# Every second ELU gate on GpSimd, the first two head pairs in written order, the first queries loaded through ScalarE's queue, and five smaller weight-decoding buffers, in a fused top-k attention and ELU feed-forward kernel

## The chip, the cores and the metric

The kernel runs on one core of one Trainium2 chip. Its measure is the device time of one launch in microseconds (us). The core has four engines that compute, each with its own instruction stream that runs in order: PE (TensorE, the matmuls; PEld are its weight loads, which overlap with them), DVE (VectorE), ACT (ScalarE) and POOL (GpSimd). SP (SyncE) issues the DMAs of the kernel before. The engines meet only in semaphores: an instruction that waits holds up all that stands behind it on its engine.

## The reference, cut to what matters

```python
q, k, v: (8, 8, 576, 64)        # batch, heads, sequence, head dim
scores = (1/8) * q @ k.T
kth    = 32nd largest of each row
scores = where(scores >= kth, scores, -1e9)
attn   = softmax(scores)
x      = (attn @ v) as (4608, 512)
h      = x @ w_in               # (512, 2048)
g      = where(h > 0, h, exp(min(h, 0)) - 1)
out    = g @ w_out              # (2048, 512), fp32
```

All inputs but q, k and v come as float64 words: the two weight matrices are passed as pairs of 32-bit words and turned into fp32 on the chip.

## The kernel before

A step is 128 query rows of one head pair. There are 144 steps: 8 batches of 4 query tiles by 4 head pairs, and 2 more for the remaining 64 rows of each batch. The life of a step `u` is spread over the loop at L640: `scores(u)` is issued two steps ahead (PE matmuls L300 into the two PSUM tiles `wide`, copied and scaled by ACT at L308); `select`, or `select_row` in the first eight steps, finds the 32 largest of each row on DVE: for each of the two heads four MAX8 (L341, L353; L319, L329 in `select_row`) and three MATCH_REPLACE8 (L346; L323) over 576 columns. One step later `mask` takes two tiny POOL operations (`neg` L366, `gap` L368), then two ACT passes (L369, L370); `normalise` takes five tiny POOL operations (L380 to L385) and two POOL passes over 576 columns (L387). Then `turn` transposes the weights on PE (L406, copied by ACT at L407) and `attend` multiplies with v (L432); `finish` copies the result into the block's `xT` (L459).

The feed-forward part works on blocks of one to three slots of 128 tokens: five blocks of one slot in the first pair of batches, otherwise blocks of two and three. For each block `ffn_pieces` makes 16 pieces `hidden(f)` (four times two matmul records each, L490; three ACT passes, L502 to L504, into `n` and `gT`; the entry in the list `gates`) and four pieces `project(s, part)` for each slot (L513, eight matmul records each, from `gT` and `w_out`). The gate itself, `gT = gT + (n - 1)`, is one DVE scalar_tensor_tensor at L471, issued by `close_gates`: `feed`, called four times a step, closes the gates that were put in the list at least two calls before; `project` closes all that are left; `hidden` closes the oldest when more than three are open. There are 304 gates (19 blocks of 16). `feed` also decides from due times which pieces are issued where; these numbers are the same in both kernels.

The weights are decoded in 32 pieces of 128 x 512 numbers. `load_weight` (SP DMA of 512 KB into a tile of pool `raw`, three buffers of 4 x 512 words), `convert_first` (three ACT passes L169 to L171, one POOL tensor_scalar L172), `convert_last` (two DVE passes L179, L182, and one POOL integer add L186). `decode_piece(i)` asks for load i+2, does the first half of piece i and the last half of piece i-1. `hook` runs one of them four times a step inside `select_row`, so that they fill steps 0 to 7 (one more falls into step 8). When the last is issued, the pools of the decoding are closed and the late pools `f` (five buffers of `n`), `g` and `x` are opened in their place.

The order on PE, ACT, DVE and POOL is a scheduler's up to step 8 (`tight`); from there `manual_schedule` keeps the order as written. SP's stream holds all loads and stores: q and k of head pair 0, two weight pieces, q and k of head pair 1, v of pair 0, then the rest.

Of the kernel before, what the change touches and what calls it, by code (L numbers as in the profile page):

```python
# [8 lines left out]
AF = mybir.ActivationFunctionType  # L9
ALU = mybir.AluOpType  # L10
FP32 = mybir.dt.float32
U32 = mybir.dt.uint32
I32 = mybir.dt.int32
# [67 lines left out]
def kernel(  # L81
# [9 lines left out]
    nc = tc.nc  # L91
    P = nc.NUM_PARTITIONS
# [16 lines left out]
    def pool(name, bufs, **kw):  # L109
        return ctx.enter_context(tc.tile_pool(name=name, bufs=bufs, **kw))  # L110
# [5 lines left out]
    wkpool = pool("wk", 1)  # L116
    etpool = pool("et", 2)
    small = pool("small", 4)
    xtpool = pool("xt", 2)
    opool = pool("o", 1)  # L120
    ps_sc = pool("ps_sc", 1, space=PSUM)
    ps_t = pool("ps_t", 2, space=PSUM)
# [3 lines left out]
    raws = ExitStack()  # L126
    early = raws.enter_context(tc.tile_pool(name="early", bufs=1))
    earlyf = raws.enter_context(tc.tile_pool(name="earlyf", bufs=4))
    rawpool = raws.enter_context(tc.tile_pool(name="raw", bufs=3))

    ident = const.tile([P, P], FP32, tag="ident", name="ident")
    make_identity(nc, ident[:])
# [15 lines left out]
        return moe_w_out[f * P : (f + 1) * P, :], w_out[:, f, :]  # L148

    def load_weight(i):  # L150
        t = rawpool.tile([P, 4 * WN], U32, tag="raw", name="raw")
        nc.sync.dma_start(t[:, 0 : 2 * WN], weight(i)[0])
        raw[i] = t

    def parts(t):
        words = t[:, 0 : 2 * WN].rearrange("p (n w) -> p n w", w=2)
        return words[:, :, 0], words[:, :, 1], t[:, 2 * WN : 3 * WN], t[:, 3 * WN :]

    def convert_first(i):

        lo, hi, e, m = parts(raw[i])
        ef, mf = e.bitcast(FP32), m.bitcast(FP32)
        nc.scalar.activation(ef, hi.bitcast(FP32), AF.Abs, scale=2.0**-48)  # L169
        nc.scalar.activation(mf, lo, AF.Copy, scale=2.0**-29, bias=2.0**23)  # L170
        nc.scalar.activation(m.bitcast(I32), mf, AF.Copy, bias=-(2.0**23))  # L171
        nc.gpsimd.tensor_scalar(  # L172
            ef, ef, (2.0 - 2.0**-3 - 2.0**-23) * 2.0**-32, 2.0**-63, ALU.min, ALU.max
        )

    def convert_last(i):
        t, dst = raw.pop(i), weight(i)[1]
        lo, hi, e, m = parts(t)
        nc.vector.tensor_scalar(  # L179
            e, e, 0x0FFFFFFF, 3, ALU.bitwise_and, ALU.logical_shift_left  # L180
        )
        nc.vector.scalar_tensor_tensor(  # L182
            out=e, in0=hi, scalar=0x80000000, in1=e,
            op0=ALU.bitwise_and, op1=ALU.bitwise_or,
        )
        nc.gpsimd.tensor_tensor(  # L186
            dst.bitcast(I32), e.bitcast(I32), m.bitcast(I32), ALU.add
        )

    decode = []  # L190
# [2 lines left out]
    def hook():  # L193

        if not decode:
            return
        decode.pop(0)()
        if not decode:
            raws.close()
            late["f"] = ctx.enter_context(tc.tile_pool(name="f", bufs=5))  # L200
            late["g"] = ctx.enter_context(tc.tile_pool(name="g", bufs=2))
            late["x"] = ctx.enter_context(tc.tile_pool(name="x", bufs=2))

    def decode_piece(i):
        if i < 2 * NF:
            if i + 2 < 2 * NF:
                load_weight(i + 2)
            convert_first(i)
        if i > 0:
            convert_last(i - 1)  # L210
            decoded[0] = i

    loaded, kqT, vT = {}, {}, {}

    def load_qk(b, hp):

        for name, src in (("k", k), ("q", q)):
            n = J + 1 if name == "k" else J
            t = ldpool.tile([P, n, 2, D], FP32, tag=name + "in", name=name + "in")
            if name == "k":  # L220
                last = t
            for hh in range(2):
                nc.sync.dma_start(
                    t[:, 0:J, hh, :],
                    src[b, 2 * hp + hh, 0:JP, :].rearrange("(p j) d -> p j d", j=J),
                )
            nc.sync.dma_start(
                last[0:R, J, :, :] if name == "k" else last[R:P, J, :, :],
                src[b, 2 * hp : 2 * hp + 2, JP:S, :].rearrange("h p d -> p h d"),
            )  # L230
            loaded[b, hp, name] = t
# [47 lines left out]
    def start_qk(b, hp):  # L279
        turning.append(transpose_qk(b, hp))  # L280
# [171 lines left out]

    def finish(blk, parts, at, cols, src):
        if blk.xT is None:
            if blk.slots == 1 and late:
                blk.xT = late["x"].tile([P, NC, P], FP32, tag="xT", name="xT")
            else:
                blk.xT = xtpool.tile([P, NC, T], FP32, tag="xT", name="xT")
        nc.scalar.copy(blk.xT[:, at, cols], src)  # L459
        blk.left -= parts  # L460
        if blk.left == 0:
            ffn.extend(ffn_pieces(blk))
# [1 line left out]
    gates = []  # L464
    place = [0]

    def close_gates(keep=0):

        while gates and gates[0][0] <= place[0] - keep:
            _, dst, n = gates.pop(0)  # L470
            nc.vector.scalar_tensor_tensor(  # L471
                out=dst, in0=n, scalar=-1.0, in1=dst, op0=ALU.add, op1=ALU.add
            )

    def ffn_pieces(blk):
        n_tok = blk.slots * P

        def hidden(f):
            if f == 0 and blk.number == 0:
                g = early.tile([P, NF, P], FP32, tag="g", name="gT")  # L480
                blk.gT = [g[:, 0:NG], g[:, NG:NF]]
            elif f % NG == 0 and blk.number > 0:
                g = late["g"].tile([P, NG, T], FP32, tag="g", name="gT")
                blk.gT.append(g[:])
            if len(gates) > 3:
                gates[0] = (-1, *gates[0][1:])
                close_gates(place[0])
            ps = ps_f.tile([P, dm], FP32, tag="f", name="hps")
            for i in range(NC):
                nc.tensor.matmul(  # L490
                    ps[:, 0:n_tok],
                    w_in[:, i, f * P : (f + 1) * P],
                    blk.xT[:, i, 0:n_tok],
                    start=(i == 0),
                    stop=(i == NC - 1),
                )
            if blk.number == 0:
                n = earlyf.tile([P, P], FP32, tag="n", name="n")[:]
            else:
                n = late["f"].tile([P, T], FP32, tag="n", name="n")[:, 0:n_tok]  # L500
            g = blk.gT[f // NG][:, f % NG, 0:n_tok]
            nc.scalar.activation(n, ps[:, 0:n_tok], AF.Relu, scale=-1.0)  # L502
            nc.scalar.activation(g, ps[:, 0:n_tok], AF.Relu)  # L503
            nc.scalar.activation(n, n, AF.Exp, scale=-1.0)  # L504
            gates.append((place[0], g, n))

        def project(s, part):
            close_gates()
            if part == 0:
                blk.o = ps_f.tile([P, dm], FP32, tag="f", name="ops")  # L510
            step = NF // 4
            for f in range(part * step, (part + 1) * step):
                nc.tensor.matmul(  # L513
                    blk.o[:],
                    blk.gT[f // NG][:, f % NG, s * P : (s + 1) * P],
                    w_out[:, f, :],
                    start=(f == 0),
                    stop=(f == NF - 1),
                )
            if part == 3:  # L520
                o = opool.tile([P, dm], FP32, tag="osb", name="osb")
                nc.scalar.copy(o[:], blk.o[:])
                for t in blk.tiles[s]:
                    p0 = t.cols.start - s * P
                    nc.sync.dma_start(out[t.rows, :], o[p0 : p0 + t.ql, :])

        part = HIDDEN[blk.slots]
        behind = 2 * NF if blk.number else 0
        return [
            (part, max(behind, NC * (f // 4 + 1)), lambda f=f: hidden(f))  # L530
            for f in range(NF)
        ] + [
            (PROJECT, max(behind, NF + (part + 1) * NF // 4),
             lambda s=s, part=part: project(s, part))
            for s in range(blk.slots)
            for part in range(4)
        ]
# [75 lines left out]
            fed["sum"] += cost  # L613
            piece()

    load_qk(0, 0)
    for i in range(2):
        load_weight(i)
    load_qk(0, 1)
    load_v(0, 0)  # L620
    start_qk(0, 0)
    turn_qk(True)
    scores(steps[0])
    load_qk(0, 2)
    start_qk(0, 1)
    turn_qk(True)
    scores(steps[1])
    load_qk(0, 3)
    for hp in range(1, NHP):
        load_v(0, hp)  # L630
    decode += [lambda i=i: decode_piece(i) for i in range(2 * NF + 1)]
    at(0, start_qk, 0, 2)
    at(1, start_qk, 0, 3)

# [5 lines left out]
    for n in range(NS + 3):  # L640
# [20 lines left out]
                feed(n, 0.25)  # L661
            continue
        if n == tight:
            E = mybir.EngineType
            ctx.enter_context(
                tc.manual_schedule(engines={E.PE, E.Activation, E.DVE, E.Pool})
            )
        passes = select(cur) if cur else iter(range(4))
        if ahead:
            scores(ahead)  # L670
# [59 lines left out]
```

## Time and profile before

| what | us |
|---|---|
| three runs, median (lowest to highest) | 1694.59 (1694.2 to 1695.28) |
| the profiled execution, its own time | 1695.23 |
| the profiled execution, first to last instruction (span) | 1693.4 |
| busy in the span: PE / DVE / ACT / POOL | 1597.5 / 1542.7 / 1179.6 / 627.0 |
| granted TensorE clock, mean | 0.974 |

Times inside the profile count from the first instruction; they are of one execution. The ends of steps used below are the ends of every eighth MAX8 on DVE: step 1 ends at 35.3 us, step 8 at 164.5, step 67 at 772.1 and step 143, the last, at 1594.3. "Busy" is the union of an engine's instructions; a busy PE is not a PE at its peak, since matmuls are pipelined and one that waits for its operands can count as busy. In the groups of instructions a row reads: line, engine, operation, output tile from input tiles, shape, count, then busy time in us, mean ns of one, and the idle time of the engine just before them with what ended it.

### The profile page before, as it was taken

How to read it: one execution, taken by the hardware profiler on the slowest of the kernel's cores; microseconds unless marked ns; L12 is line 12 of the kernel's file. 1: busy time of each engine (PE TensorE's matmuls, PEld its weight loads, DVE VectorE, ACT ScalarE, POOL GpSimd, SP SyncE). 2: the span in 40 equal slices, each digit the busy share in tenths (PEclk: the TensorE clock that was granted, in tenths of full speed). 3: DMA queues.
4: the chain of work that ended last, by engine and by line, in shares of the span. 5: the costliest groups of instructions: out<-in, count | busy, mean ns of one | idle time of the engine just before them, and what ended most of it. 6: DMA issues, size and time to landing. Idle time of an engine off the chain costs nothing.

```text
span 1693.4 us, 26805 instructions
## 1 busy us (share of the span) xinstructions
PE 1597.5 (94%) x8560; PEld 1035.0 (61%) x8560; DVE 1542.7 (91%) x3248; ACT 1179.6 (70%) x2813; POOL 627.0 (37%) x1719
## 2 busy tenths in 40 slices
PE   4568899999999999999999999999999999999999
PEld 3355676667575666756557575755557575755565
DVE  6889999999999999999999999999998999998600
ACT  5787776778776776857758585867758686857531
POOL 3675333343333333433333333333333333332200
PEclk8568999999999999999999999999999999999999
DMA  5531021001200111001100111001100000000000
GB/s 156 169 130 63 15 56 36 7 1 42 51 12 7 29 35 42 1 14 42 43 19 1 28 42 35 7 10 46 36 20 8 21 21 28 7 7 7 7 13 13
DMA packets 101131, 56.25 MB, mean 33 GB/s; under 512 B 84096, under 2 KB 92288, under 8 KB 100992
## 3 DMA queue, kind: packets, MB, share of 16 engines
q1 hardware_dynamic: 100992, 54.55, 11.7%
q8 instruction: 68, 1.11, 0.3%
q14 instruction: 71, 0.58, 0.1%
HBM read 45.09 MB, written 9.44 MB: 32 GB/s over the span
## 4 chain that ended last, share of the span: by engine, by line
PE 68%; DVE 21%; ACT 5%; issue 2%; POOL 2%; DMA 1%; SPq 0%; ACTq 0%; POOLq 0%; DVEq 0%
PE ops L513 25%; PE hps L490 21%; PE avps L432 8%; DVE wk L346 7%; PE scps L300 7%; DVE m L353 6%; PE eps L406 5%; DVE m L341 2%; DVE gT L471 1%; DVE wk L323 1%; DVE m L329 1%; PE qkps L270 1%; ACT sc L370 1%; ACT sc L369 1%; ACT et L407 1%
## 5 line engine op out<-in xcount | busy, mean ns | idle before, releaser
L353 DVE MAX8 m<-wk 128x8 f32<-128x576 f32 x816 | 574.9, 745 | 0.0
L490 PE MATMUL hps<-xT,w_in 128*128 128x256 f32 (+2 forms) x2432 | 554.3, 376 | 19.3 <-ACT gT L503 19.3
L513 PE MATMUL ops<-w_out,gT 128*128 128x512 f32 x1152 | 522.6, 598 | 0.0
L490 PEld LDWEIGHTS hps<-xT,w_in 128*128 128x128 f32 x2432 | 409.5, 194 | 119.9 <-ACT gT L503 26.4
L346 DVE MATCH_REPLACE8 wk<-m,wk 128x576 f32<-128x576 f32 x544 | 399.4, 741 | 0.0
L513 PEld LDWEIGHTS ops<-w_out,gT 128*128 128x128 f32 x1152 | 208.4, 190 | 232.8 <-issue 201.0
L380 POOL TENSOR_SCALAR dene<-den 128x2 f32<-128x2 f32 x144 | 34.9, 243 | 819.6 <-ACT sc L370 819.0
L369 ACT ACTIVATE sc<-sc,neg 128x576 f32<-128x576 f32 x288 | 226.5, 787 | 56.6 <-POOL neg L366 56.1
L370 ACT ACTIVATE sc<-sc,gap 128x576 f32<-128x576 f32 x288 | 223.2, 775 | 26.6 <-ACT sc L369 1.9
L308 ACT ACTIVATE sc<-scps 128x576 f32<-128x576 f32 x288 | 173.4, 661 | 82.4 <-PE scps L300 82.4
L387 POOL TENSOR_SCALAR sc<-sc,rec 128x576 f32<-128x576 f32 x288 | 218.7, 769 | 15.2 <-POOL rec L385 0.4
L300 PE MATMUL scps<-kqT 64*128 64x288 f32 (+1 forms) x1280 | 198.1, 438 | 21.5 <-ACT sc L308 14.7
L471 DVE SCALAR_TENSOR_TENSOR gT<-n,gT 128x256 f32<-128x256 f32 (+2 forms) x304 | 129.1, 431 | 95.3 <-ACT n L504 95.3
L407 ACT COPY et<-eps 128x512 f32<-128x512 f32 x288 | 167.4, 581 | 61.8 <-PE eps L406 61.8
L406 PEld LDWEIGHTS eps<-ident,sc 128*128 128x128 f32 x1152 | 144.5, 145 | 93.4 <-issue 48.9
L346 DVE MATCH_REPLACE8 wk<-m,sc 128x576 f32<-128x576 f32 x272 | 199.7, 741 | 0.0
L432 PE MATMUL avps<-et,vT 128*64 128x256 f32 (+2 forms) x2080 | 191.0, 325 | 9.0 <-ACT et L407 8.4
L406 PE MATMUL eps<-ident,sc 128*128 128x128 f32 x1152 | 177.9, 280 | 21.8 <-POOL sc L387 18.6
L341 DVE MAX8 m<-sc 128x8 f32<-128x576 f32 x272 | 191.3, 744 | 0.0
L432 PEld LDWEIGHTS avps<-et,vT 128*64 128x64 f32 x2080 | 122.3, 140 | 80.4 <-issue 24.7
L502 ACT ACTIVATE n<-hps 128x256 f32<-128x256 f32 (+2 forms) x304 | 112.6, 370 | 84.2 <-PE hps L490 79.0
L300 PEld LDWEIGHTS scps<-kqT 64*128 64x128 f32 (+1 forms) x1280 | 106.0, 180 | 90.2 <-issue 45.1
(47 smaller groups left out, 1236.6 us busy)
## 6 DMA issues: line engine op xcount, KB each, us to landing
kin<-in_k_dram SPq DMA_DIRECT2D x64, 128.0 KB, 2.8
qin<-in_q_dram SPq DMA_DIRECT2D x64, 128.0 KB, 2.8
raw<-in_moe_w_in_dram SPq DMA_DIRECT2D x16, 512.0 KB, 3.9
vT<-in_v_dram SPq DMA_DIRECT2D x64, 128.0 KB, 2.3
raw<-in_moe_w_out_dram SPq DMA_DIRECT2D x16, 512.0 KB, 3.3
out_dram<-osb SPq DMA_DIRECT2D x32, 256.0 KB, 2.2
kin<-in_k_dram SPq DMA_DIRECT2D x32, 32.0 KB, 2.5
kin<-in_q_dram SPq DMA_DIRECT2D x32, 32.0 KB, 2.2
```

What stands on the lines that cost most here:

```text
L300: nc.tensor.matmul(wide[i][rows, half, 0:HS], kq[part, q0 : q0 + u.t.ql], kq[part, k0 : k0 + HS], start=True, stop=True,)
L341: nc.vector.max(found[i], cur[i])
L346: nc.vector.match_replace(wk[i], found[i], cur[i], TAKEN)
L353: nc.vector.max(found[i], cur[i])
L369: nc.scalar.activation(sc, sc, AF.Prelu, bias=neg[:], alpha=STEEP)
L370: nc.scalar.activation(sc, sc, AF.Exp, bias=gap[:], accum_out=u.den[:, i : i + 1])
L387: nc.gpsimd.tensor_scalar(u.sc[:, i, :], u.sc[:, i, :], rec[:, i : i + 1], 1.0, ALU.mult, ALU.mult)
L406: nc.tensor.transpose(ps[:, c * P : (c + 1) * P], sc[:, c0 : c0 + P], ident[:])
L407: nc.scalar.copy(g.et[:, chunks, u.at, :], ps[:, 0 : n * P].rearrange("p (c q) -> p c q", c=n),)
L432: nc.tensor.matmul(ps[i * D : (i + 1) * D, cols], vt[:, 2 * J + i if c == J else i * J + c, :], w, start=(c == 0), stop=(c == J),)
L490: nc.tensor.matmul(ps[:, 0:n_tok], w_in[:, i, f * P : (f + 1) * P], blk.xT[:, i, 0:n_tok], start=(i == 0), stop=(i == NC - 1),)
L513: nc.tensor.matmul(blk.o[:], blk.gT[f // NG][:, f % NG, s * P : (s + 1) * P], w_out[:, f, :], start=(f == 0), stop=(f == NF - 1),)
```

## The change

In the decoding: the tile `raw` loses its fourth part (the rounded low words are written over `lo`, with every second word of the tile as target), and the pool has five buffers of 3 x 512 words; the last half of a piece is done two pieces after its first half instead of one, so there is one more `decode_piece`. In the prologue: the first query loads (three DMAs) are issued by ACT's queue; weight piece 0 is asked for ahead of head pair 1, and piece 1 behind it; transposes and scores of both first head pairs are issued under `manual_schedule`, ahead of the loads of pairs 2 and 3. In the gates: the gates of odd f are closed on POOL by two instructions (subtract one from `n` in place, then add into `gT`); `project` closes only the gates that its part reads. In the pools: `n` has four late buffers instead of five; `xT` of one-slot blocks has three buffers from the start, and the two buffers of wider blocks are opened late.

```diff
-    xtpool = pool("xt", 2)
+    xpool = pool("x", 3)
...
-    rawpool = raws.enter_context(tc.tile_pool(name="raw", bufs=3))
+    rawpool = raws.enter_context(tc.tile_pool(name="raw", bufs=5))
...
-        t = rawpool.tile([P, 4 * WN], U32, tag="raw", name="raw")
+        t = rawpool.tile([P, 3 * WN], U32, tag="raw", name="raw")
...
-        return words[:, :, 0], words[:, :, 1], t[:, 2 * WN : 3 * WN], t[:, 3 * WN :]
+        return words[:, :, 0], words[:, :, 1], t[:, 2 * WN :]
...
-        ef, mf = e.bitcast(FP32), m.bitcast(FP32)
+        ef, mf = e.bitcast(FP32), lo.bitcast(FP32)
         nc.scalar.activation(ef, hi.bitcast(FP32), AF.Abs, scale=2.0**-48)
         nc.scalar.activation(mf, lo, AF.Copy, scale=2.0**-29, bias=2.0**23)
-        nc.scalar.activation(m.bitcast(I32), mf, AF.Copy, bias=-(2.0**23))
+        nc.scalar.activation(lo.bitcast(I32), mf, AF.Copy, bias=-(2.0**23))
...
-            dst.bitcast(I32), e.bitcast(I32), m.bitcast(I32), ALU.add
+            dst.bitcast(I32), e.bitcast(I32), lo.bitcast(I32), ALU.add
...
-            late["f"] = ctx.enter_context(tc.tile_pool(name="f", bufs=5))
+            late["f"] = ctx.enter_context(tc.tile_pool(name="f", bufs=4))
             late["g"] = ctx.enter_context(tc.tile_pool(name="g", bufs=2))
-            late["x"] = ctx.enter_context(tc.tile_pool(name="x", bufs=2))
+            late["x"] = ctx.enter_context(tc.tile_pool(name="xt", bufs=2))
...
             convert_first(i)
-        if i > 0:
-            convert_last(i - 1)
-            decoded[0] = i
+        if i > 1:
+            convert_last(i - 2)
+            decoded[0] = i - 1
...
-    def load_qk(b, hp):
+    def load_qk(b, hp, other=nc.sync):
...
-            n = J + 1 if name == "k" else J
+            n, queue = (J + 1, nc.sync) if name == "k" else (J, other)
...
-            if blk.slots == 1 and late:
-                blk.xT = late["x"].tile([P, NC, P], FP32, tag="xT", name="xT")
+            if blk.slots == 1:
+                blk.xT = xpool.tile([P, NC, P], FP32, tag="xT", name="xT")
             else:
-                blk.xT = xtpool.tile([P, NC, T], FP32, tag="xT", name="xT")
+                blk.xT = late["x"].tile([P, NC, T], FP32, tag="xT", name="xT")
...
-    def close_gates(keep=0):
+    def close_gates(keep=0, upto=None):
...
-        while gates and gates[0][0] <= place[0] - keep:
-            _, dst, n = gates.pop(0)
-            nc.vector.scalar_tensor_tensor(
-                out=dst, in0=n, scalar=-1.0, in1=dst, op0=ALU.add, op1=ALU.add
-            )
+        while gates:
+            put, group, dst, n = gates[0]
+            if put > place[0] - keep if upto is None else group > upto:
+                return
+            gates.pop(0)
+            if group[1] % 2 == 0:
+                nc.vector.scalar_tensor_tensor(
+                    out=dst, in0=n, scalar=-1.0, in1=dst, op0=ALU.add, op1=ALU.add
+                )
+            else:
+                nc.gpsimd.tensor_scalar_add(n, n, -1.0)
+                nc.gpsimd.tensor_tensor(dst, dst, n, ALU.add)
...
-                gates[0] = (-1, *gates[0][1:])
-                close_gates(place[0])
+                close_gates(upto=gates[0][1])
...
-            gates.append((place[0], g, n))
+            gates.append((place[0], (blk.number, f), g, n))
...
-            close_gates()
+            close_gates(upto=(blk.number, (part + 1) * NF // 4 - 1))
...
-    load_qk(0, 0)
-    for i in range(2):
-        load_weight(i)
+    E = mybir.EngineType
+    engines = {E.PE, E.Activation, E.DVE, E.Pool}
+    load_qk(0, 0, nc.scalar)
+    load_weight(0)
     load_qk(0, 1)
+    load_weight(1)
     load_v(0, 0)
-    start_qk(0, 0)
-    turn_qk(True)
-    scores(steps[0])
+    with tc.manual_schedule(engines=engines):
+        for hp in range(2):
+            start_qk(0, hp)
+            turn_qk(True)
+            scores(steps[hp])
     load_qk(0, 2)
-    start_qk(0, 1)
-    turn_qk(True)
-    scores(steps[1])
     load_qk(0, 3)
...
-    decode += [lambda i=i: decode_piece(i) for i in range(2 * NF + 1)]
+    decode += [lambda i=i: decode_piece(i) for i in range(2 * NF + 2)]
```

More of the change, by code (lines that the diff above doesn't have):

```diff
@@ L156, in parts @@
         words = t[:, 0 : 2 * WN].rearrange("p (n w) -> p n w", w=2)
-        return words[:, :, 0], words[:, :, 1], t[:, 2 * WN : 3 * WN], t[:, 3 * WN :]
+        return words[:, :, 0], words[:, :, 1], t[:, 2 * WN :]
     def convert_first(i):
-        lo, hi, e, m = parts(raw[i])
-        ef, mf = e.bitcast(FP32), m.bitcast(FP32)
+        lo, hi, e = parts(raw[i])
+        ef, mf = e.bitcast(FP32), lo.bitcast(FP32)
         nc.scalar.activation(ef, hi.bitcast(FP32), AF.Abs, scale=2.0**-48)
         nc.scalar.activation(mf, lo, AF.Copy, scale=2.0**-29, bias=2.0**23)
-        nc.scalar.activation(m.bitcast(I32), mf, AF.Copy, bias=-(2.0**23))
+        nc.scalar.activation(lo.bitcast(I32), mf, AF.Copy, bias=-(2.0**23))
         nc.gpsimd.tensor_scalar(
@@ L177, in convert_last @@
         t, dst = raw.pop(i), weight(i)[1]
-        lo, hi, e, m = parts(t)
+        lo, hi, e = parts(t)
         nc.vector.tensor_scalar(
@@ L222, in load_qk @@
             for hh in range(2):
-                nc.sync.dma_start(
+                queue.dma_start(
                     t[:, 0:J, hh, :],
@@ L226, in load_qk @@
                 )
-            nc.sync.dma_start(
+            queue.dma_start(
                 last[0:R, J, :, :] if name == "k" else last[R:P, J, :, :],
@@ L663 @@
         if n == tight:
[L664 to L667, printed above, removed]
+            ctx.enter_context(tc.manual_schedule(engines=engines))
         passes = select(cur) if cur else iter(range(4))
```

## The prediction, made before the changed kernel ran

> **What bounds the kernel now.** I read the page first: the share of each engine, then the slices.
>
> ```profile
> PE 1597.5 (94%) x8560; PEld 1035.0 (61%) x8560; DVE 1542.7 (91%) x3248; ACT 1179.6 (70%) x2813; POOL 627.0 (37%) x1719
> ...
> PE   4568899999999999999999999999999999999999
> DVE  6889999999999999999999999999998999998600
> ...
> PEclk8568999999999999999999999999999999999999
> ```
>
> Two engines are near full, so an average says nothing on what a gate is worth. The second view is the busy time of each engine in five stretches, cut at ends of steps: two steps of prologue; seven with decoding; steps 9 to 67; 68 to 143; the tail.
>
> ```profile
> core 0: us, PE busy (x) PEld busy (x) DVE busy (x) ACT busy (x) POOL busy (x), PEclk, DMA share, GB/s
> 0.00:35.30 35.30, 16.11 (x80) 11.41 (x81) 22.71 (x45) 17.32 (x34) 9.91 (x32) 0.89 0.68 179
> 35.30:164.50 129.20, 87.12 (x419) 60.80 (x418) 115.79 (x217) 98.36 (x225) 88.11 (x137) 0.70 0.39 121
> 164.50:772.10 607.60, 581.01 (x3548) 394.01 (x3547) 607.60 (x1312) 449.90 (x1132) 225.40 (x669) 1.00 0.10 25
> 772.10:1594.30 822.20, 818.25 (x4195) 513.38 (x4192) 789.82 (x1662) 586.45 (x1352) 296.93 (x864) 1.00 0.08 22
> 1594.30:1693.40 99.10, 94.97 (x329) 55.35 (x327) 6.82 (x17) 27.61 (x73) 6.68 (x18) 1.00 0.04 14
> ```
>
> DVE has no gap at all from 164.5 to 772.1: there it sets the pace, with PE 26.6 us short of full. From 772.1 PE sets it (818.25 of 822.20) and DVE has 32 us to spare. In the decoding DVE is idle for 13.4 us of 129.2, and the groups and waits say on what: the chain DMA, ACT, POOL of a weight piece.
>
> ```profile
> L179 DVE TENSOR_SCALAR raw<-raw 128x512 uint32<-128x512 uint32 x30 | 19.9, 662 | 12.7 <-POOL raw L172 12.7
> ...
> L182 DVE SCALAR_TENSOR_TENSOR raw<-raw 128x512 uint32<-128x512 uint32 x30 | 22.5, 750 | 0.0
> ...
> SPq L152 <- POOL w_out L186: 39.0, 10, 7.2
> SPq L152 <- POOL w_in L186: 28.4, 10, 4.6
> ```
>
> The last two (SP's own waits) say that the load of a piece stood for 67.4 us behind the POOL add that frees one of three buffers.
>
> **The change, part by part.** *Gates.* Half of 304 leave DVE. What one is worth is read from two neighbouring steps, one with no gate and one with three of 128x256:
>
> ```profile
> 464.24:473.88 9.64, 9.64 (x34) 4.85 (x35) 9.64 (x22) 5.31 (x11) 3.75 (x14) 1.00 0.11 31
> 483.52:494.17 10.65, 10.65 (x63) 8.31 (x60) 10.65 (x25) 7.79 (x21) 2.50 (x10) 1.00 0.00 1
> ```
>
> (10.65 - 9.64)/3 = 0.34 us, less than the 0.42 of its own row, as its end overlaps the next instruction. Steps 9 to 67 hold 59 x 9.64 = 568.8 us of selection, so the other 607.6 - 568.8 = 38.8 us are the 131 gates of the groups there; half is -19.4 us. PE could give more: its 26.6 us of idle time lie above that, but not by much.
>
> On POOL a gate is two instructions that no row shows at this size. The one-input form: L387 takes 748 ns for 576 columns, L172 612 for 512 when nothing meets it, L366 235 for one; 256 columns about 0.42 us. The two-input form: L186 takes 1272 for 512 and L368 200 for one, so 200 + 256 x 2.09 = 0.74. Between them a semaphore, as between L380 and L382 (12.0 us before 144, 0.08). Sum 1.24 us; bounds: 0.40 (two tiny ones) and 1.9 (both at 512). On POOL 152 x 1.24 = 188 us, on 627. What hides it: POOL is idle 819.0 us ahead of L380, waiting for ACT, that is 5.7 us a step against 1.06 x 1.24 = 1.3. So I take it as nothing by itself. Queued behind a POOL gate are neg and gap of the next mask (ACT waits for neg: 56.1 us today, 46 times) and the normalise that PE's transposes wait for; if the cover were gone, up to all of the 1.24 would lie on that chain.
>
> What it does cost is collisions on DVE, which this trace shows while POOL decodes:
>
> ```profile
> 37.99 0.43 DVE L179 TENSOR_SCALAR raw<-raw 128x512 uint32<-128x512 uint32 x1 [2.04 <-POOL raw L172]
> ...
> 40.23 1.27 POOL L186 TENSOR_TENSOR w_in<-raw 128x512 int32<-128x512 int32 x1
> 40.33 1.45 DVE L179 TENSOR_SCALAR raw<-raw 128x512 uint32<-128x512 uint32 x1
> ```
>
> The same DVE pass takes 0.43 us alone and 1.45 beside the two-input POOL add. The 16 gates in the decoding stretch mean 648 ns, the 64 of the same size after it 302. MAX8 and MATCH_REPLACE8 stay at 741 to 746 ns whatever POOL does, so only the remaining DVE gates can be hit, each for at most the POOL add's 0.74. With 1.1 POOL gates a step of 10.3 us, placed at random, a DVE gate of 0.41 meets an add in 1.1 x (0.41 + 0.74)/10.3 = 12% and loses half of 0.74; a little more for the subtraction: 0.09 us. On 65 gates +6 us (bounds 0 and 65 x 0.74 = 48). Net -13.4 us here. In steps 68 to 143, PE's 4 us of idle time are all that can be won: -1. The gates of the tail lie beside PE's last projections.
>
> One rule speaks against this part: the Trainium skill, GPSIMD Engine Reference, section Engine selection, keeps elementwise work on VectorE and calls GpSimd about 2x slower with two inputs. The rows agree on the ratio (L186 1272 ns, L182 670 unhindered). By the rule alone the part would be a loss of some 152 x (1.24 - 0.41) = 126 us of engine time; by the stretches that time falls on an engine idle for 60% of the span, so the sum above stands.
>
> *Project closing only its own gates, four n buffers, the xT pools:* nothing. DVE has no gate wait in the stretch it bounds; its 95.3 us of waits for ACT's exponent lie where PE bounds. A fifth n buffer matters only if a gate is still open four pieces later; `feed` closes after two calls (5 us) and some one piece is issued a call. Without that cover ACT's L502 waits for a gate just issued, 0.4 to 1.2 us a piece.
>
> *Decoding.* The load no longer waits for the add of the piece before last: with three buffers, a piece goes through DMA (3.9 us to landing), ACT, POOL, DVE, POOL in some 13 us, which at three pieces allows one in 4.3 us; steps 2 to 7 take 22.7, 20.9, 18.8, 19.2, 17.3 and 16.9 us with four pieces each. With five buffers, and the DVE half one piece later, the 12.7 us that DVE waits for L172 should mostly go: I take -10 (bounds 0 and -13.4, all idle time of the stretch). It is not more, since the DVE passes remain and still meet L186: 30 x (0.66 + 0.75) = 42 us with some 10 of collisions in it. Gates here: 16 of 10.3 us, half to POOL: -5, of which I give back 3, since POOL (88.1 of 129.2) gets eight gates more. Low words in place: L171 would read and write every second word like L170, 671 for 628 ns, 1.4 us of ACT, hidden by its 31 us of idle time.
>
> *Prologue.* Today the first scores stand behind the third k DMA of head pair 1, issued at 7.19 and landed at 12.39 (the chain: 5.87 us from 6.52), and MAX8 starts at 15.91. Removed: three query issues on SP (1.9 us) and the pair-1 transposes ahead of the scores. Added: in the built order ACT runs piece 0 (2 us) ahead of the kqT copies and two passes of piece 1 ahead of the score copies, and DVE both passes of piece 1 ahead of MAX8. Piece 1 now stands behind both head pairs: 2.18 MB where today 1.89 MB had landed by 12.39, some 190 GB/s; so 13.9 us. Then 0.67 (L169), 0.61 (L172), 1.1 on DVE: MAX8 at 16.3, +0.4 us (bounds -3 and +5, the latter if loads run at the 149 GB/s of 15.9 to 25.7).
>
> Decoding and prologue together: -10 - 2 + 0.4, and +3.6 for a denser decoding that collides more, -8 (bounds -18 and +8).
>
> **Sum.** -13.4 - 1 - 8 = -22.4 on a span of 1693.4: 1671.0. The execution's own time was 1.8 us over its span, 1672.8, and 0.6 over the median of the runs: 1672.
>
> **The rivals.** *PE takes over everything* (0.17): no collisions, prologue and decoding at their best: -19.4 - 4 - 16 gives 1655. For it: all three bounds are rows; against: collisions are in the trace. *Only the gates pay* (0.17): decoding just moves from waiting for L172 to colliding with L186, or a late piece 1 eats its gain: -14.4, so 1680; with the prologue's +5, 1685. For it: ACT and POOL are already 76% and 68% busy there. *Only the decoding pays* (0.05): 96% busy PE takes over in steps 9 to 67 at once, 1686. *Slower: the two halves of the gates meet* (0.12). Place: steps 9 to 67, where `close_gates` issues neighbouring f to DVE and POOL; if both are released together, each DVE gate waits 0.74: 65 x 0.74 = 48 against 19.4 won, +28.7; with -1 and -8, 1714. It decides from 0.6 of the gates: 28.4/48. Against: POOL's queue is paced by ACT's exponents, DVE's by selection, and L387, long as it is, meets few gates today. *It does not do what it says:* the built order has 152 subtract and add pairs on POOL; below 0.01, counted with the last.
>
> **Numbers.** The forecast, 1662 to 1686, has 0.48. The range 1656 to 1691 takes in most of the first three rivals and leaves out about 0.2. A change below 0.2% (3.4 us) can't be told from none here. Faster 0.81: 0.48 + 0.17 + 0.16 of the next two; same 0.07, their rest and a mild collision; slower 0.12.
>
> **What would show it.** Right: steps without a gate still 9.64 us, steps 40 to 44 some 0.4 shorter; DVE no longer full from step 9 on while PE rises above 97%; step 8 ends by 158; L179's wait for L172 below 4 us; POOL near 820 us. Wrong: mean DVE gates of 128x256 above 0.6 us (collisions), ACT's wait for neg well above 56 us (POOL in the way), MAX8 starting after 18 us, steps 2 to 7 still at 19.

## The result and the profile after

The changed kernel is slower: 1708.2 us, median of four runs (1707.29 to 1709.38), against 1694.93 for the kernel before on the same chip; ratio 1.0079, 95% interval 1.0061 to 1.0096. The profiled execution took 1707.29 us with a span of 1705.5, where before's span was 1693.4. The forecast of 1672, its range and its sign were wrong.

The page of the changed kernel, with the shares of the engines, two rows of slices, and the chain that ended last:

```profile
PE 1602.6 (94%) x8560; PEld 1032.1 (61%) x8560; DVE 1497.1 (88%) x3096; ACT 1178.2 (69%) x2813; POOL 851.9 (50%) x2023
...
PE   4568999999999999999999999999999999999999
...
DVE  6899999999999999998989899998997989897500
...
PE 67%; ACT 15%; POOL 7%; DVE 5%; issue 3%; SPq 1%; DMA 1%; ACTq 0%; POOLq 0%
```

What was to leave DVE left it: 1542.7 us busy before, 1497.1 now. The chain shows what came in its place; before it was:

```profile
PE 68%; DVE 21%; ACT 5%; issue 2%; POOL 2%; DMA 1%; SPq 0%; ACTq 0%; POOLq 0%; DVEq 0%
```

DVE held 21% of it, ACT 5% and POOL 2%; now DVE holds 5%, ACT 15% and POOL 7%.

The same five stretches, cut at the ends of steps 1, 8, 67 and 143 (columns as in the prediction):

```profile
0.00:35.30 35.30, 18.91 (x85) 12.56 (x85) 22.46 (x46) 20.81 (x40) 11.16 (x34) 0.95 0.73 202
35.30:159.40 124.10, 80.20 (x404) 56.49 (x405) 114.13 (x207) 94.67 (x219) 92.48 (x146) 0.72 0.39 119
159.40:771.10 611.70, 582.47 (x3534) 392.76 (x3533) 591.07 (x1247) 446.69 (x1125) 307.62 (x801) 1.00 0.09 25
771.10:1605.10 834.00, 824.81 (x4208) 514.24 (x4207) 766.03 (x1592) 587.58 (x1357) 421.37 (x1010) 1.00 0.08 21
1605.10:1705.50 100.40, 96.22 (x334) 56.08 (x332) 3.40 (x8) 28.50 (x76) 19.31 (x34) 0.99 0.04 14
```

| stretch | before | after | difference | predicted |
|---|---|---|---|---|
| prologue and decoding, to the end of step 8 | 164.5 | 159.4 | -5.1 | -8 |
| steps 9 to 67 | 607.6 | 611.7 | +4.1 | -13.4 |
| steps 68 to 143 | 822.2 | 834.0 | +11.8 | -1 |
| tail | 99.1 | 100.4 | +1.3 | 0 |

DVE has lost its lead in steps 9 to 67 (591.07 of 611.70 us busy), and still the stretch is longer. The larger loss lies in steps 68 to 143, where PE set the pace before and DVE had time to spare.

The waits of the whole changed kernel (us in total, times, longest):

```profile
POOL dene L381 <- ACT sc L371: 648.9, 137, 10.4
DVE gT L478 <- ACT n L513: 150.6, 46, 44.2
ACT sc L370 <- POOL neg L367: 104.6, 60, 6.8
...
DVE raw L180 <- POOL raw L173: 22.4, 10, 9.2
```

POOL is still idle 648.9 us ahead of its normalisation, so its busy share says that there is room. But ACT's wait for `neg`, the first tiny POOL operation of a mask, has gone from 56.1 us to 104.6. The line of before:

```profile
ACT sc L369 <- POOL neg L366: 56.1, 46, 3.3
```

In steps 68 to 143 alone, before and then after:

```profile
ACT sc L369 <- POOL neg L366: 19.0, 17, 3.3
```

```profile
ACT sc L370 <- POOL neg L367: 50.7, 29, 5.5
...
PE avps L433 <- ACT et L408: 4.1, 7, 1.6
```

PE's wait for ACT's `et` was 0.2 us there before. One case from the timeline of the changed kernel, in step 33 (start, duration, engine and line, and in brackets the idle time before it with its releaser):

```profile
409.61 1.68 POOL L388 TENSOR_SCALAR sc<-sc,rec 128x576 f32<-128x576 f32 x2
...
411.27 0.86 POOL L482 TENSOR_SCALAR n<-n 128x256 f32<-128x256 f32 x1
...
412.21 0.73 POOL L483 TENSOR_TENSOR gT<-gT,n 128x256 f32<-128x256 f32 x1
...
412.91 0.23 POOL L367 TENSOR_SCALAR neg<-m 128x1 f32<-128x1 f32 x1
...
413.17 0.78 ACT L370 ACTIVATE sc<-sc,neg 128x576 f32<-128x576 f32 x1 [2.35 <-POOL neg L367]
...
415.01 0.59 ACT L277 COPY kqT<-qkps 128x512 f32<-128x512 f32 x1
...
415.65 0.66 PE L407 MATMUL eps<-ident,sc 128*128 128x128 f32 x4 [0.44 <-ACT kqT L277]
```

The gate runs on POOL between the normalisation and the next `neg` (411.27 to 412.94 us). ACT, which takes its work in order, stands for 2.35 us, and the gate's 1.67 lie inside them; the copies of `kqT` queued behind its masks come later for it, and PE waits 0.44 us for one of them. This is one case; that it is the cause had to be tested.

### The profile page after: what moved, and what is told of

Read it like the earlier page. It is cut to its first block, busy times and chain, and to the rows that moved or that the text cites. A ratio compares the mean times of both kernels' runs of the same rounds, so it can differ in the third digit from the quotient of the medians.

```text
span 1705.5 us, 26881 instructions
## 1 busy us (share of the span) xinstructions
PE 1602.6 (94%) x8560; PEld 1032.1 (61%) x8560; DVE 1497.1 (88%) x3096; ACT 1178.2 (69%) x2813; POOL 851.9 (50%) x2023
## 3 DMA queue, kind: packets, MB, share of 16 engines
q1 hardware_dynamic: 99792, 54.26, 11.5%
q8 instruction: 68, 1.11, 0.3%
## 4 chain that ended last, share of the span: by engine, by line
PE 67%; ACT 15%; POOL 7%; DVE 5%; issue 3%; SPq 1%; DMA 1%; ACTq 0%; POOLq 0%
PE ops L522 28%; PE hps L499 17%; PE avps L433 9%; PE scps L301 6%; PE eps L407 5%; ACT sc L371 4%; ACT sc L370 4%; ACT et L408 2%; POOL sc L388 2%; DVE wk L347 1%; ACT n L511 1%; ACT n L513 1%; ACT gT L512 1%; POOL n L482 1%; DVE m L354 1%
## 5 line engine op out<-in xcount | busy, mean ns | idle before, releaser
L381 POOL TENSOR_SCALAR dene<-den 128x2 f32<-128x2 f32 x144 | 33.9, 235 | 649.5 <-ACT sc L371 648.9
L370 ACT ACTIVATE sc<-sc,neg 128x576 f32<-128x576 f32 x288 | 226.5, 787 | 104.9 <-POOL neg L367 104.6
L388 POOL TENSOR_SCALAR sc<-sc,rec 128x576 f32<-128x576 f32 x288 | 213.8, 752 | 14.9
L433 PE MATMUL avps<-et,vT 128*64 128x256 f32 (+2 forms) x2080 | 195.9, 325 | 18.2 <-ACT et L408 18.0
L408 ACT COPY et<-eps 128x512 f32<-128x512 f32 x288 | 167.0, 580 | 56.3 <-PE eps L407 56.1
L478 DVE SCALAR_TENSOR_TENSOR gT<-n,gT 128x256 f32<-128x256 f32 (+2 forms) x152 | 68.8, 452 | 153.9 <-ACT n L513 150.6
## 6 DMA issues: line engine op xcount, KB each, us to landing
kin<-in_k_dram SPq DMA_DIRECT2D x64, 128.0 KB, 2.8
vT<-in_v_dram SPq DMA_DIRECT2D x64, 128.0 KB, 2.3
qin<-in_q_dram SPq DMA_DIRECT2D x62, 128.0 KB, 2.8
```

What stands on the lines that cost most here:

```text
L370: nc.scalar.activation(sc, sc, AF.Prelu, bias=neg[:], alpha=STEEP)
L388: nc.gpsimd.tensor_scalar(u.sc[:, i, :], u.sc[:, i, :], rec[:, i : i + 1], 1.0, ALU.mult, ALU.mult)
L408: nc.scalar.copy(g.et[:, chunks, u.at, :], ps[:, 0 : n * P].rearrange("p (c q) -> p c q", c=n),)
L433: nc.tensor.matmul(ps[i * D : (i + 1) * D, cols], vt[:, 2 * J + i if c == J else i * J + c, :], w, start=(c == 0), stop=(c == J),)
```

## The experiments

Three theories stood at the start. The queue (Q): a POOL gate stands ahead of `neg` and so of ACT and PE. Collisions (C): POOL's gates slow DVE's instructions. Late closing (L): `project` that closes only its own gates, with four buffers of `n`, lets gates come late. The runs are called e1 to e11. Spans and stretches below are of the profiled execution of each run; ratios are to the kernel before, with the 95% interval in brackets.

**e1. All gates back on DVE**, the rest of the change as it is.

```diff
-            if group[1] % 2 == 0:
+            if True:
```

> The changed kernel with every gate on DVE again; prologue, decoding, pools and the late closing of gates stay. Theory Q (a POOL gate's time stands in POOL's queue ahead of the next neg, gap and normalise, and holds ACT and then PE): only the 5 us of the front are left of the change, 1688 to 1691. Theory C (DVE and POOL gates collide): the same 1688 to 1691. Theory L (closing gates late, with four buffers of n, makes the loss): 1700 or more.

Measured 1692.99 us, ratio to before 0.9995 (0.9985 to 1.0005). That is 2 us above what Q and C gave and far from L's 1700. So the change without its POOL gates is the kernel before, within what can be measured: with the gates on DVE, closing and buffers cost nothing. The loss comes with the POOL gates.

**e2. The POOL gates alone in the kernel before**, with its own closing and five buffers of `n`.

```diff
-            _, dst, n = gates.pop(0)
...
+            _, odd, dst, n = gates.pop(0)
+            if odd:
+                nc.gpsimd.tensor_scalar_add(n, n, -1.0)
+                nc.gpsimd.tensor_tensor(dst, dst, n, ALU.add)
...
```

> The kernel before with one edit: gates of odd f on POOL by the same two instructions, closed where they were closed before, five buffers of n. Q and C: 1705 to 1716, the loss without the gain of the front. L: 1680 to 1696, since nothing is closed later.

Measured 1717.15 us, 1.0134 (1.0118 to 1.0149): slower than the whole change, and slower than either theory said. The POOL gates do the harm without the change's other parts. The stretches show where the other parts soften it: steps 2 to 8 take 133.9 us here and 124.1 in the changed kernel, and DVE waits there 21.7 us for POOL's L172 against 9.7. Steps 9 to 67 and 68 to 143 take 612.1 and 833.9 us, as in the changed kernel (611.7 and 834.0), though gates are closed earlier and `n` has five buffers: L falls for POOL gates too. So next to POOL gates the other parts are worth some 10 us in the decoding, where without POOL gates they bring nothing that can be measured (e1); which of them it is was not tried.

**e3. The subtraction in another form**: one instruction with two operations in place of one.

```diff
-                nc.gpsimd.tensor_scalar_add(n, n, -1.0)
+                nc.gpsimd.tensor_scalar(n, n, -1.0, 1.0, ALU.add, ALU.mult)
```

> The changed kernel with the subtraction on POOL written in the form with two operations (add -1, times 1), as the normalise at L388 has it, whose 576 columns take 748 ns; the form of the change takes 871 ns for 256. If the form makes the difference, a POOL gate falls from 1.6 to about 1.1 us. Q: a third of the loss goes, 1698 to 1705. C: collisions with the add stay, 1705 to 1709. L: 1708. If the form makes no difference, the mean stays at 871 and the time at 1708 under all three.

Measured 1696.3 us, 1.0016 (1.0007 to 1.0026). The groups of the changed kernel, then of this run (count, busy us, mean ns, idle before):

```profile
L482 POOL TENSOR_SCALAR n<-n 128x256 f32<-128x256 f32 x88 | 76.8, 873 | 39.5 <-ACT n L513 39.5
L483 POOL TENSOR_TENSOR gT<-gT,n 128x256 f32<-128x256 f32 x88 | 65.0, 739 | 7.3
L478 DVE SCALAR_TENSOR_TENSOR gT<-n,gT 128x256 f32<-128x256 f32 x88 | 40.8, 464 | 122.3 <-ACT n L513 119.0 <-POOL gT L483 3.1
```

```profile
L483 POOL TENSOR_TENSOR gT<-gT,n 128x256 f32<-128x256 f32 x88 | 64.1, 728 | 7.3
...
L482 POOL TENSOR_SCALAR n<-n 128x256 f32<-128x256 f32 x88 | 36.2, 411 | 43.8 <-ACT n L513 43.8
```

The one-operation form takes 873 ns where the same result takes 411 in the two-operation form. Over all 152 gates POOL's time falls from 238.0 us (1.57 each) to 169.2 (1.11), and the span by 11.6. The run is faster than either theory gave. The time on POOL counts; whether in its queue or by collisions, this run does not say.

**e4. The odd gates left out.**

```diff
-            else:
-                nc.gpsimd.tensor_scalar_add(n, n, -1.0)
-                nc.gpsimd.tensor_tensor(dst, dst, n, ALU.add)
```

> The changed kernel without the gates of odd f: half of the ELU's last step (the exponential part of odd hidden chunks) is left out, all else stays. What the prediction counted on if POOL's work were free: 1665 to 1680 under Q and C (13 to 20 us less in steps 9 to 67, 5 in the front). L: 1695 or more, since the even gates are still closed late.

Measured 1682.89 us, 0.9934 (0.9919 to 0.9948), 3 us above what Q and C gave. Two readings. The POOL gates cost 1705.5 - 1681.4 = 24.1 us of span. And even where half the gates cost nothing at all, steps 9 to 67 shrink only from 608.9 us (all gates on DVE, e1) to 601.4: -7.5, not -19.4.

**e5. The same POOL gates in another place**: from step 8 on odd gates are held back to the third `feed` of a step, behind `neg` and `gap` of the second mask and ahead of `normalise`, in the two-operation form. The third `feed` also closes even gates one call earlier than before.

```diff
...
-        close_gates(2)
+        close_gates(2, odd=False)
+        if odd:
+            close_gates(1)
...
-        feed(n, 0.25)
+        feed(n, 0.25, False)
```

> The two-operation form of e3, and the POOL gates issued at one place of a step alone: behind neg and gap of the second row, ahead of the normalise, where POOL waits for ACT's Exp anyway (649 us ahead of L381 in the changed kernel). Same POOL work, same DVE work, one call to feed later or earlier. Theory Q (queue): with nothing ahead of neg, most of the 12 us between e3 (1696) and the kernel without odd gates (1683) go, 1683 to 1688. Theory C (collisions on the port): as many collisions, 1694 to 1698.

Measured 1685.91 us, 0.9948 (0.9934 to 0.9963), faster than both kernels. POOL's gates take 169 us as in e3, and yet the span is 1685.2 against 1693.9. Its waits:

```profile
POOL dene L381 <- ACT sc L371: 549.2, 137, 10.5
POOL n L481 <- ACT n L514: 195.7, 70, 24.0
...
ACT sc L370 <- POOL neg L367: 49.0, 36, 6.8
```

POOL now waits 195.7 us with a gate at the head of its queue, and that costs little, since what comes next is a normalisation, not a `neg`. ACT's wait for `neg` is back at 49.0. The earlier even gates are not tried by themselves, but they can hardly be the gain: in the changed kernel no wait of PE is put down to a DVE gate, and ACT waits 2.2 us for one.

**e6. That place with the one-operation form**, so that POOL's work is that of the changed kernel again.

```diff
-                nc.gpsimd.tensor_scalar(n, n, -1.0, 1.0, ALU.add, ALU.mult)
+                nc.gpsimd.tensor_scalar_add(n, n, -1.0)
```

> The place of e5 with the subtraction in the change's form (871 ns). Q: the form matters little when the time lies in POOL's wait for Exp, 1684 to 1692, against 1708 with the change's places. C or plain length of the gate: 1704 to 1710.

Measured 1687.66 us, 0.9958 (0.9943 to 0.9973); span 1686.3. Its waits:

```profile
POOL n L481 <- ACT n L514: 166.1, 68, 24.0
...
ACT sc L370 <- POOL neg L367: 51.7, 37, 6.8
```

POOL's gates take 236 us, as in the changed kernel, and 19.2 us of the 24.1 are gone. The POOL instructions are the same and differ in place: that is Q. C as the main cause falls, since the collisions stayed: DVE's 152 gates together take 68.7 us in the changed kernel, 67.4 here, and 67.8 in e4 where no POOL gate can meet them.

**e7. Gates of one column on POOL** (the rest of each odd gate is left out): the same waits and order, hardly any time.

```diff
-                nc.gpsimd.tensor_scalar_add(n, n, -1.0)
-                nc.gpsimd.tensor_tensor(dst, dst, n, ALU.add)
+                nc.gpsimd.tensor_scalar_add(n[:, 0:1], n[:, 0:1], -1.0)
+                nc.gpsimd.tensor_tensor(dst[:, 0:1], dst[:, 0:1], n[:, 0:1], ALU.add)
```

> The changed kernel with the POOL gates over one column instead of all (the rest of the odd gates is left out): the waits for ACT's exponent and the places in the queue stay, their 1.6 us become about 0.5. If the time that a gate takes in the queue is what costs, 24 us x 0.5/1.6 = 8 over the kernel without odd gates, 1686 to 1692. If the wait for the exponent at the head of POOL's queue costs, 1700 or more.

Measured 1685.3 us, 0.9947 (0.993 to 0.9964), just below the first range; span 1683.0. A POOL gate that waits for its exponent with `neg` behind it is nearly harmless (+1.6 us of span over e4); the length of the gate does the harm. In this place 66.5, 169.2 and 238.0 us of POOL gates (this run, e3, the changed kernel) cost 1.6, 12.5 and 24.1 us of span: some 10% of the longest. ACT's wait for `neg` grows with them: 46.5 us in e4 without POOL gates, then 55.4, 82.4 and 104.6.

**e8. The decoding alone** in the kernel before (five smaller buffers, last half two pieces later, and the pool sizes that make room for them).

```diff
-    rawpool = raws.enter_context(tc.tile_pool(name="raw", bufs=3))
+    rawpool = raws.enter_context(tc.tile_pool(name="raw", bufs=5))
...
-        if i > 0:
-            convert_last(i - 1)
-            decoded[0] = i
+        if i > 1:
+            convert_last(i - 2)
+            decoded[0] = i - 1
...
```

> The kernel before with the decoding edits alone: five buffers of three parts, the last half two pieces later, and the pool sizes that make room for them; gates on DVE, prologue as before. By the prediction's term of -10 us for the decoding: 1684 to 1687. By what the kernel with all gates on DVE showed (125.9 us in steps 2 to 8 for 129.2): 1690 to 1694.

Measured 1693.53 us, 0.9996 (0.9986 to 1.0005): nothing that can be told from none. Steps 2 to 8 take 128.0 us against 129.2.

**e9. The prologue alone** in the kernel before.

```diff
-    load_qk(0, 0)
-    for i in range(2):
-        load_weight(i)
+    load_qk(0, 0, nc.scalar)
+    load_weight(0)
     load_qk(0, 1)
+    load_weight(1)
...
+    with tc.manual_schedule(engines=engines):
+        for hp in range(2):
+            start_qk(0, hp)
+            turn_qk(True)
+            scores(steps[hp])
...
```

> The kernel before with the prologue's edits alone: pair 0's queries on ACT's DMA queue, the new load order, the head pairs in written order; gates, closing, buffers and decoding as before. The prediction's term for it is +0.4 us, so about 1695. The rival reading, from the step ends of the changed kernel (its first MAX8 starts at 14.97 us, before's at 15.91), is that the front's gain of some 1 us is this edit's: 1693 to 1694. In the trace the first reading wants the first MAX8 at 16 us or later, the second at about 15 us.

Measured 1695.44 us, 1.0006 (0.9996 to 1.0015). Again nothing. The first MAX8 starts at 15.63 us, between the two readings (before 15.91, after 14.97).

**e10. No gates at all**, neither on DVE nor on POOL.

```diff
             gates.pop(0)
-            if group[1] % 2 == 0:
...
-            else:
-                nc.gpsimd.tensor_scalar_add(n, n, -1.0)
-                nc.gpsimd.tensor_tensor(dst, dst, n, ALU.add)
```

> The changed kernel without any gate: the second half of the ELU of every hidden tile is left out, on VectorE too (the even ones) and on GpSimd (the odd ones). It prices what the gates can give at most. If VectorE's work still sets the pace of steps 9 to 67 once the odd gates are gone (run e4, 1682.9 us), taking the rest, about as much again (19 us by the prediction's division), gives another 7 to 19 us: 1664 to 1676. If the chain through ScalarE and TensorE sets it there by then, it stays near e4: 1676 to 1683, with VectorE's busy time in steps 9 to 67 well under that stage's length.

Measured 1682.63 us, 0.9936 (0.9919 to 0.9952): the time of e4. Taking away the other half of the gates gains nothing. The last three stretches, first of e4 and then of this run:

```profile
158.10:759.50 601.40, 579.26 (x3545) 393.57 (x3545) 589.85 (x1246) 448.11 (x1129) 222.90 (x672) 1.00 0.10 25
759.50:1580.80 821.30, 817.38 (x4199) 512.41 (x4196) 765.07 (x1591) 587.55 (x1355) 289.87 (x867) 1.00 0.08 22
1580.80:1681.40 100.60, 96.44 (x334) 56.20 (x332) 3.40 (x8) 27.57 (x73) 6.68 (x18) 1.00 0.04 13
```

```profile
156.40:739.80 583.40, 561.65 (x3469) 382.82 (x3468) 570.51 (x1182) 434.21 (x1097) 215.73 (x660) 1.00 0.10 25
739.80:1561.20 821.40, 817.48 (x4208) 513.91 (x4207) 739.17 (x1521) 592.08 (x1366) 281.59 (x861) 1.00 0.09 23
1561.20:1680.70 119.50, 115.27 (x404) 66.14 (x402) 0.03 (x1) 37.79 (x96) 12.89 (x37) 1.00 0.04 11
```

DVE's steps 9 to 67 do get 18.0 us shorter, but the tail gets 18.9 longer: DVE finishes its selection earlier, with more of PE's matmuls still to do (404 records after its end, not 334). Stretches cut at DVE's steps measure DVE, and only the sum shows that PE did not follow.

**e11. The placed gates in the kernel before**, with its own prologue, decoding, pools and closing (e5's gates, in the two-operation form, and e5's place).

```diff
...
-        close_gates(2)
+        close_gates(2, odd=False)
+        if odd:
+            close_gates(1)
...
```

> The kernel before, with its own prologue, decoding, pools and closing, and one thing changed: the gates of odd f run on GpSimd as in run e5, in the two-operation form and at the third feed of a step, behind the tiny operations of the next mask and ahead of the normalisation. If the gates alone hold what is to be had (the parts beside them measured as nothing in e1, e8 and e9), it comes within 3 us of e5's 1685.9: 1683 to 1689. If the denser decoding is needed for it (e5's steps 2 to 8 took 124.5 us, before's 129.2), it keeps those 4.7 us: 1690 to 1693. GpSimd's time per gate should stay about 1.11 us and ScalarE's wait for neg about 50 us in both.

Measured 1688.82 us, 0.9969 (0.9957 to 0.998). ACT's wait for `neg` is 41.8 us. This lies at the top of the first range: most of e5's gain is the gates' own. The rest (the profiled spans are 1687.1 and 1685.2) is too small to be told from nothing: the intervals of the two ratios overlap.

## Why the prediction was wrong

**What half the gates are worth: wrong, -7.5 in place of -19.4.** The arithmetic per step was sound. In the changed kernel steps without a gate still take 9.64 us, step 41 fell from 10.65 to 10.01 and step 44 from 10.64 to 9.97; but step 40 rose from 10.65 to 13.01, so that steps 40 to 44 together took 1.0 us more, not 2 less. PE did not rise above 97% either: 582.47 of 611.70 us are 95%. What failed is the reading of "DVE has no gap at all from 164.5 to 772.1: there it sets the pace", and of PE's 26.6 us of idle time as room that DVE's relief would fill. PE's own waits in steps 9 to 67, in the kernel before, e4 and e10, in that order:

```profile
PE hps L490 <- ACT gT L503: 16.2, 20, 1.6
```

```profile
PE hps L496 <- ACT gT L509: 14.6, 21, 1.6
```

```profile
PE hps L492 <- ACT gT L505: 14.2, 19, 1.6
```

More than half of PE's idle time there ended on ACT, which empties the hidden layer's PSUM tiles, and it stays so whatever DVE does: 26.6 us idle before, 601.40 - 579.26 = 22.1 with half the gates gone, 583.40 - 561.65 = 21.8 with none. DVE, relieved, meets that same chain: in e4 it stands 11.5 us in this stretch at gates whose exponent ACT has not made. Step 40, the first of a group with hidden pieces, shows it: 12.53 us even in e4, 2.0 of them at such gates, which eats most of what the next steps gain.

**"I take it as nothing by itself": wrong, +24.1 us.** This is the step that turned the sign. The cover named, POOL's 819.0 us of idle time ahead of the normalisation, is an average and lies after `neg`, not before it. The prediction named the queue (neg, gap, normalise behind a gate), and even the mark that would show it, ACT's wait for `neg` above 56 us, but gave it no price and no rival. Its bound, all of the gate's time on that chain, would have been 152 x 1.24 = 188 us; a tenth of the real time sufficed.

**The size of a POOL gate: 1.57 us (mean of all 152) for 1.24.** At 256 columns the add was right (0.74), the subtraction 0.87 for 0.42. L387 (times `rec`, times 1.0) and L172 (min, max), taken as its rows, are two-operation forms; the one-operation form has its own price, and before's only rows of it are of one or two columns (L366, L380). The two-operation form made the same place 11.6 us cheaper.

**Collisions: far smaller than reckoned.** DVE's gates of 128x256 take 464 ns in the changed kernel and the same 88 gates 440 in e4, some 24 ns each where 90 were reckoned; over all of its 152 gates DVE loses about 1 us (68.7 against 67.8). The slower rival (two halves meet, 1714) came near in time by luck: its cause is not there, and DVE waits for a POOL gate once, for 3.1 us.

**Decoding, -10: wrong, between -2.4 and +0.8.** The interval of e8 is that. DVE's wait for L172 was only partly the load's: in steps 2 to 8 it is 11.3 us in e8 and 9.7 in the changed kernel, for 12.7 before. Here is its longest piece in the changed kernel:

```profile
52.18 0.23 POOL L381 TENSOR_SCALAR dene<-den 128x2 f32<-128x2 f32 x1
...
54.15 1.48 POOL L388 TENSOR_SCALAR sc<-sc,rec 128x576 f32<-128x576 f32 x2
...
55.71 1.20 POOL L173 TENSOR_SCALAR raw<-raw 128x512 f32<-128x512 f32 x2
...
56.36 0.83 DVE L180 TENSOR_SCALAR raw<-raw 128x512 uint32<-128x512 uint32 x1 [2.70 <-POOL raw L173]
```

The piece's POOL operation stands behind a whole normalisation (52.18 to 55.63 us): in this case POOL's order again, not the number of buffers. The mark "below 4 us" had said that this would show. Only beside POOL gates does the record show a worth of the other parts in this stretch (e2).

**Prologue, +0.4; closing and pools, nothing: not contradicted.** e9 gives +1.0 with nothing inside its interval; e1 gives -1.3 for closing, pools, decoding and prologue together, with nothing inside it too. MAX8 was forecast at 16.3 us; it starts 0.7 earlier in e9 and 1.3 earlier in the changed kernel. Why these two differ was not looked into.

**Steps 68 to 143, -1: wrong, +11.8.** With the odd gates left out they take 821.3 us, and 822.7 with the same POOL instructions in e6's place, so nearly the whole of it is POOL's gates ahead of `neg`; PE, busy 818 of 822 us before, has little room to take up a late mask.

**The rule that spoke against the part.** The prediction set aside the Trainium skill's GPSIMD Engine Reference, section Engine selection, which keeps elementwise work on VectorE. Its verdict held for the change (1708.2 us against e1's 1692.99), but not through the rate alone: with the same instructions in another place (e6, 1687.66) the version with GpSimd gates beats e1.

**A version that beats both**: e5, 1685.91 us, 3 us above the run that leaves the odd gates out.

## What to carry to other kernels

Work moved to an idle engine is priced by what stands behind it in that engine's queue, not by the engine's idle share: look for the slot whose next instruction nobody is waiting for. And before crediting relief of a full engine, ask what ends the waits of the engine that fills the span; if it is a third engine, the relief stops there. A stretch cut at one engine's steps measures that engine alone, so check the last stretch for work that was only pushed on.

## What the runs showed of the hardware that was not expected

On POOL a tensor_scalar with one operation (add -1, in place, float32) took 556, 873 and 1249 ns at 128, 256 and 384 columns in the changed kernel; with a second operation that changes nothing (multiply by 1) 303, 411 and 568 ns in e3. That is (1249 - 556)/256 = 2.7 ns a column against 1.0. At one column the one-operation form took 238 ns in e7, about what `neg` takes. Why the shorter request is the slower was not tried.
